# Sliding-window attention and a two-layer product on one core: full products for the first chunk, scores one unit at a time, and a stored order for every engine

## The chip, the cores and the metric

One core of a Trainium2 chip. The time is the device time of one execution in microseconds (us), median of the runs named. "Span" is the time from the first to the last instruction in the profiled execution, which lies 1.6 to 1.8 us below that run's own time. "Clock" is the granted clock of TensorE as a share of full speed. PE is TensorE, DVE is VectorE, ACT is ScalarE, POOL is GpSimd. Products of PE land in PSUM (tiles named ps); the other on-chip tiles lie in SBUF. An evacuation copies or combines a finished product out of PSUM. All quoted times are of runs in the fast state unless said otherwise; a run in the slow state is named and left out of the ratios.

## The reference, cut to what matters

```python
# q, k, v: 8 batches x 8 heads x 576 positions x 64;  w_in: 512x2048;  w_out: 2048x512
scores = scale * q @ k^T                       # ALiBi bias, causal window of 128
attn   = softmax(where(mask, scores + bias, -1e9))
x      = (attn @ v).transpose(0, 2, 1, 3).reshape(4608, 512)
h      = x @ w_in                              # "MoE1" in the texts below
g      = h * np.cos(h)
out    = g @ w_out                             # "MoE2"
```

## The kernel before

The kernel collects operations with their dependencies, then a scheduler gives each engine its order. PE needs attention (scores, then P·V, which multiplies the softmax weights by v), MoE1 and MoE2 for nine chunks of 512 tokens, and mixes them so that one fills the waits of another. MoE2 of every chunk is done with seven block products in place of eight, which needs sums of weight blocks (once) and of activation blocks (per chunk). Three of the four weight sums run on DVE, the fourth on GpSimd:

```python
def weight_sums():
    B11, B12 = w_out[:, 0:HF, 0:256], w_out[:, 0:HF, 256:512]
    B21, B22 = w_out[:, HF:NFC, 0:256], w_out[:, HF:NFC, 256:512]
    ...
    for o, i0, i1, r, w in (
            (T[1][:, :, :], B12, B11, up, [("T", 1)]),
            (T[2][:, :, :], B22, T[1][:, :, :], low + [("T", 1)], [("T", 2)]),
            (B12, B22, B12, low, up),                       # overwrites the weights
            (T[4][:, :, :], B21, T[2][:, :, :], low + [("T", 2)], [("T", 4)])):
        eng = "pool" if w == [("T", 4)] else "dve"
        op(eng, ... e.tensor_tensor(o, i0, i1, ALU.subtract) ...)
```

After the exponential, a mask is multiplied in on DVE:

```python
op("dve", lambda e, p=p, m=m: e.tensor_tensor(p, p, m, ALU.mult), ...)   # p, emask: SBUF, bf16
```

Two units of attention (a unit is a batch, a pair of heads and a group of rows) take their scores in one run on PE, in a mode that uses 64 of its rows (64*128 in the traces):

```python
scores(two, 0)                       # mode=1: both units in one run of matmuls
for n, u in enumerate(two):
    exps(u, n, 2 * phase + 2)
```

The order is made by a greedy list scheduler: at each step it takes, over all engines, the operation that can start first by modelled durations, with priorities where several can.

```python
while avail:
    ...
    soon = min(st for st, _ in cand)
    st, o = min(((st, o) for st, o in cand
                 if st <= soon + (40 if e != "pe" else 100 if o.pri < 5 else 10)),
                key=lambda c: (c[1].pri, c[1].seq))
```

The softmax here doesn't subtract the row's maximum and nothing guards it: scores larger than these inputs give would overflow.

## Time and profile before

| | before |
|---|---|
| median of 3 runs | 321.86 us (320.95 to 323.0) |
| span of the profiled run | 318.1 us, clock 0.987 (this run took 319.88 us) |
| PE busy | 293.0 us (92%), so 25.1 us idle |
| DVE, ACT, POOL busy | 259.3, 200.5, 100.9 us |

Here is one more view, the busy time by window, over four stretches of the span. The columns are: window, length, then busy time and number of instructions of PE, its weight loads, DVE, ACT and POOL, then clock, DMA share and GB/s.

```profile
37.00:58.00 21.00, 14.08 (x175) 9.64 (x174) 21.00 (x47) 11.81 (x16) 15.12 (x13) 0.84 1.31 110
58.00:80.00 22.00, 20.64 (x154) 11.98 (x154) 18.78 (x36) 15.29 (x23) 11.92 (x16) 1.00 1.93 140
80.00:284.00 204.00, 200.82 (x1954) 135.94 (x1964) 169.83 (x378) 138.60 (x195) 54.31 (x65) 1.00 1.09 112
284.00:318.10 34.10, 28.30 (x246) 23.44 (x245) 21.63 (x39) 5.81 (x11) 0.00 (x0) 0.98 0.26 86
```

Read length minus PE busy. PE idles 6.92 us in the first stretch, where DVE is full and the clock is 0.84 on average; 1.36 in the second, 3.18 in the long middle and 5.80 in the tail. The remaining 7.8 us lie before 37 us.

### The profile page before, as it was taken

How to read it: one execution, taken by the hardware profiler on the slowest of the kernel's cores; microseconds unless marked ns; L12 is line 12 of the kernel's file. 1: busy time of each engine (PE TensorE's matmuls, PEld its weight loads, DVE VectorE, ACT ScalarE, POOL GpSimd, SP SyncE). 2: the span in 40 equal slices, each digit the busy share in tenths (PEclk: the TensorE clock that was granted, in tenths of full speed). 3: DMA queues.
4: the chain of work that ended last, by engine and by line, in shares of the span. 5: the costliest groups of instructions: out<-in, count | busy, mean ns of one | idle time of the engine just before them, and what ended most of it. 6: DMA issues, size and time to landing. Idle time of an engine off the chain costs nothing.

```text
span 318.1 us, 7293 instructions
## 1 busy us (share of the span) xinstructions
PE 293.0 (92%) x2931; PEld 204.1 (64%) x2948; DVE 259.3 (82%) x569; ACT 200.5 (63%) x287; POOL 100.9 (32%) x123
## 2 busy tenths in 40 slices
PE   2899776998999998999999999999999999997995
PEld 2677545546754776548798855676476467666884
DVE  3798999799979698789988799789977586758653
ACT  6887755694859765686768667966887651632010
POOL 8960069727993812930392040000000000000000
PEclk9999959999999999999999999999999999999999
DMA  7999999999999999999999999623102001012122
GB/s 142 179 207 208 205 83 83 164 150 121 171 145 171 155 172 186 166 152 143 200 143 156 149 133 117 93 85 99 28 0 60 19 33 68 33 34 68 66 100 100
DMA packets 148865, 38.09 MB, mean 120 GB/s; under 512 B 133984, under 2 KB 148064, under 8 KB 148832
## 3 DMA queue, kind: packets, MB, share of 16 engines
q0 software_dynamic: 99344, 18.10, 75.0%
q1 hardware_dynamic: 49488, 19.54, 33.5%
q8 instruction: 23, 0.38, 0.5%
q14 instruction: 10, 0.08, 0.1%
HBM read 36.70 MB, written 9.44 MB: 145 GB/s over the span
## 4 chain that ended last, share of the span: by engine, by line
PE 56%; DMA 18%; POOL 12%; SPq 6%; DVE 5%; issue 2%; ACT 0%; POOLq 0%; DVEq 0%; ACTq 0%
PE ps L705 26%; PE ps L819 24%; DMA w_outb<-in_moe_w_out_dram 7%; SPq L378 6%; DMA qnat<-in_q_dram 5%; DMA kt<-knat 4%; DMA knat<-in_k_dram 2%; POOL knat L367 2%; POOL vp L357 2%; POOL qnat L367 2%; PE ps L513 2%; POOL wsum L756 2%; PE ps L598 1%; PE ps L601 1%; DVE p L567 1%
## 5 line engine op out<-in xcount | busy, mean ns | idle before, releaser
L705 PE MATMUL ps<-xT,w_inb 128*128 128x512 bf16 (+1 forms) x559 | 113.2, 355 | 1.0 <-issue 0.2
L711 ACT ACTIVATE cos<-ps,halfpi 128x512 f32<-128x512 f32 x128 | 81.7, 687 | 33.4 <-DVE gT L715 20.7
L715 DVE TENSOR_TENSOR gT<-ps,cos 128x512 f16<-128x512 f32 x128 | 81.6, 685 | 12.1 <-ACT cos L711 9.7
L705 PEld LDWEIGHTS ps<-xT,w_inb 128*128 128x128 bf16 x576 | 54.9, 98 | 49.6 <-DVE gT L715 1.1
L543 ACT ACTIVATE p<-ps 128x768 bf16<-128x768 f32 (+1 forms) x64 | 55.5, 915 | 28.5 <-PE ps L513 24.2
L819 PE MATMUL ps<-w_outb,gT 128*128 128x256 f16 x432 | 56.3, 275 | 2.2 <-DVE ob L843 1.7
L357 POOL DMA_DIRECT2D vp<-in_v_dram x40 | 34.0, 901 | 50.0 <-PE ps L601 30.2
L819 PEld LDWEIGHTS ps<-w_outb,gT 128*128 128x128 f16 x432 | 40.8, 98 | 9.9 <-DVE ob L843 2.0
L567 DVE TENSOR_TENSOR p<-p,emask 128x512 bf16<-128x512 bf16 (+1 forms) x96 | 43.7, 490 | 3.3 <-ACT p L543 3.0
L819 PE MATMUL ps<-wsum,gsum 128*128 128x256 f16 x288 | 38.8, 275 | 1.2 <-ACT ob L839 0.7
L819 PEld LDWEIGHTS ps<-wsum,gsum 128*128 128x128 f16 x288 | 27.1, 98 | 7.5 <-ACT ob L839 1.0
L367 POOL DMA_DIRECT2D qnat<-in_q_dram x30 | 25.5, 896 | 13.0 <-DMA qt<-qnat 8.1
L367 POOL DMA_DIRECT2D knat<-in_k_dram x30 | 25.5, 909 | 1.9 <-DMA kt<-knat 1.9
L513 PE MATMUL ps<-qt,kt 64*128 64x128 bf16 (+1 forms) x320 | 19.8, 252 | 5.2 <-DVE gT L738 2.0
L639 DVE TENSOR_TENSOR xnat<-ps,rec 128x256 bf16<-128x256 f32 x64 | 24.3, 419 | 0.2
L598 PE MATMUL ps<-vp,p 128*128 128x65 bf16 x256 | 18.8, 196 | 3.5 <-DVE p L567 2.2
L598 PEld LDWEIGHTS ps<-vp,p 128*128 128x128 bf16 x256 | 15.9, 99 | 8.4 <-DVE p L567 3.6
L513 PEld LDWEIGHTS ps<-qt,kt 64*128 64x128 bf16 x320 | 11.8, 98 | 12.1 <-issue 4.7
L819 PE MATMUL ps<-wsum,gT 128*128 128x256 f16 x144 | 18.2, 273 | 1.1 <-DVE krows L843 1.1
L779 DVE TENSOR_TENSOR gsum<-gT 128x1024 f16<-128x1024 f16 x18 | 12.3, 684 | 8.3 <-PE ps L819 8.3
L819 PE MATMUL ps<-w_outb,gsum 128*128 128x256 f16 x144 | 18.9, 273 | 0.0
L601 PE MATMUL ps<-vp,p 128*128 128x65 bf16 x192 | 17.5, 195 | 0.0
(69 smaller groups left out, 322.6 us busy)
## 6 DMA issues: line engine op xcount, KB each, us to landing
out_dram<-ob SPq DMA_DIRECT2D x32, 256.0 KB, 3.1
vp<-in_v_dram POOLq DMA_DIRECT2D x32, 128.0 KB, 9.3
qnat<-in_q_dram POOLq DMA_DIRECT2D x24, 128.0 KB, 9.3
knat<-in_k_dram POOLq DMA_DIRECT2D x24, 128.0 KB, 11.4
w_inb<-in_moe_w_in_dram POOLq DMA_DIRECT2D x4, 512.0 KB, 10.5
w_outb<-in_moe_w_out_dram POOLq DMA_DIRECT2D x4, 512.0 KB, 22.2
out_dram<-ob SPq DMA_DIRECT2D x8, 128.0 KB, 1.7
qrows<-in_q_dram POOLq DMA_DIRECT2D x1, 576.0 KB, 15.2
```

The lines of the kernel that those rows point to most:

```text
L357: op("pool", [lambda e, t=t, rows=rows: e.dma_start(vp[b % 2][0:rows, t, :, 0:64], v[b, :, 128 * t:128 * t + rows, :].rearrange("h p d -> ...
L367: fns.append(lambda e, t=t, rows=rows: e.dma_start(nat[which][b % 2][0:rows, t, :, :], src[b, :, 128 * t:128 * t + rows, :].rearrange("h p ...
L513: ins = e.matmul(ps[:, banks[x], c0:c1], keys_ap(b, x, pr, kc), query_ap(b, x, pr, qb, 128 * nb), start=True, stop=True)
L543: op("act", lambda e: e.activation(P[i][:, :, 0:hi], src_[:, :, 0:hi], ACTF.Exp, scale=0.125), w=held + [("P", i)], occ=920 if G else 691, ...
L567: op("dve", lambda e, p=p, m=m: e.tensor_tensor(p, p, m, ALU.mult), r=[("P", i), ("EM", h0), ("EM", h1)], w=[("P", i)] if n != 1 else [("P ...
L598: ins = e.matmul(o, P[i][:, x, d0:d0 + 128], V[:, kc, h, 0:65], start=True, stop=not two)
L601: ins = e.matmul(o, P[i][:, x, p0:p0 + 128], V[:, kc - 1, h, 0:65], start=False, stop=True)
L639: op("dve", lambda e: e.tensor_tensor(o, U[:, :, :, 0:64], rv[:, :, :, None].broadcast_to([128, 2, 2, 64]), ALU.mult), r=[("rec", n % 2)], ...
L705: op("pe", lambda e, kc=kc, c0=c0: e.matmul(ps[:, bank, c0:c0 + n], w_in[:, kc, 128 * fc:128 * fc + 128], xT[:, kc, (r0 + c0) % XR:(r0 + c ...
L711: op("act", lambda e: e.activation(cosb[ci][:, :], ps[:, bank, :], ACTF.Sin, bias=halfpi[:, 0:1]), r=["halfpi"], w=[("B", bank), ("cos", c ...
L715: op("dve", lambda e: e.tensor_tensor(gT[gi][:, fc, :], ps[:, bank, :], cosb[ci][:, :], ALU.mult), r=[("cos", ci)], w=[("B", bank), ("g", ...
L819: op("pe", lambda e, t=t, fc=fc, bk=bk: e.matmul(ps[:, bk, 256 * t:256 * t + 256], lhs(fc, t), rhs(fc), start=first and fc == 0 and (last ...
```

## The change

Its intent: the first chunk's MoE2 shall not wait for sums, scores shall be free to go one unit at a time, and the greedy order gives way to an order found beforehand by a local search on the schedule model (the kernel holds the finished table). The weight sum that overwrote a block of the weights gets its own buffer, since the full products read that block. Where an instruction of DVE writes what one of the few just before it on DVE reads (fewer than four back), it gets an explicit wait.

```diff
+STARTS = ( ...  # packed start times, one for each operation
+)
     def schedule(self):
-        ...                              # the greedy scheduler
+        raw, n = zlib.decompress(base64.b85decode(STARTS)), len(self.all)
+        code = 0
+        for i, o in enumerate(self.all):
+            code = (code + 256 * raw[i] + raw[n + i]) & 0xFFFF
+            o.start = code >> 1
             if len(o.eng) > 1:
+                e = "dve" if code & 1 else "act"
+                o.fn, o.eng = o.fn[e], (e,)
+        self.order = sorted(self.all, key=lambda o: (o.start, o.seq))
...
-                if data == ORDER or self.held(d, data, e):
+                near = data == WAR and e == "dve" and len(ops[e]) - d.nth < 4
+                if data == ORDER or (self.held(d, data, e) and not near):
                     continue
...
-                    (B12, B22, B12, low, up),
+                    (T[3][:, :, :], B22, B12, up + low, [("T", 3)]),
...
+        FAST = set(range(1, NCH))
+        def moe2_plain(c):               # 4 row tiles x 16 products of 512 columns
+            ...
         def moe2(c):
+            if c not in FAST:
+                moe2_plain(c)
+                return
...
+        SINGLE = True
-                if phase < 0:
+                if phase < 0 or SINGLE:
                     for n, u in enumerate(two):
                         scores([u], n)
-                        exps(u, n, 0)
+                        exps(u, n, 2 * phase + 2)
                         mask(u)
```

More of the change, by code (lines that the diff above doesn't have):

```diff
@@ L1 @@
+import base64
 import math
+import zlib
 from contextlib import ExitStack
@@ L25 @@
 ENG = ("pe", "act", "dve", "pool", "sp")
+STARTS = (
+    "c-p;I3vg3a8qO_MkCz>|JyvZ_(l(r4TQ-Io!li9`bJK*jA-rOF^pSRJLoHA!Rf@RSf`SzaEk!^<K`Nl)QV|?sl(meD=&*`)R"
+    "bbs&U2)fOQCM{pS9vV7x%=OnN0X*VnQ_caPX5<<{NMTi??l7MvL^8HD+6dU6Hvh}E4pga1f7wecnCbFm;<V;e*K}9A`Ehj%7"
+    "oNjjjCugJ>g~jVM)GbTcnp6WZdAqy?t58aZJwuS;pYdm#3zG+Wt`5>LNc5Wtccsy>J5~GiQTaG7+0!{c|~5Wg=k@tq|C@mr="
+    "(EuN;x=&s*ey0U8VlQK}pXZeUJa4|5)zQJ&ZviMg07equx9L0Fh8fu`vLO%nr=<_e%ip2Qz}vQVy9sT}_R`zadZ4<0gN{v{="
+    "W-Z%|&0qWF0D5QQxEaez1V`Bzmi8@)RzM_EZ?K_aVX-{}}_+iv;k^9=@va*Gr(J&Xm;t$dhbBz_qTs34!PmJYqe@omzjMNij"
+    ">#N1cs$>S3`^$I-20aRM*&ptfz#>d<G|Cs^)!Muiz?ixGOH^j>)iE9*i%1&l32hap$_x{<{Cpk8_I+<e(?;`v97TNoe#O+=h"
+    "nfOnw5qunZ1Z1>5}7El;`&~eeqe#CM;))VX@eFfYWFZ!a^&9yIegwrOn}UKVw>z*+mg{-idKijpuh}NG8e9V?co~>Jr#^5_V"
+    "r~3ep#7FS^4uNU!7O4ev5-)=UAkEQmen0VWQHCVC}eQVEU4dCWhXAuU;qyAb?tqO;L_|)dIhA%xRgJ6U$*<lq2riKS1UK*@|"
+    "wJ<8#x~4M{1vpRgRqU3}YkcB<R$aJz?{v8?~#gzH#hrTkr`y!;+!^aB?*I2;aJE)3vzyLYve-)J`$k`3;a#JM=>b#Bh=mW<Y"
+    "d!p;Ay{!p)-#9idIGxyDI5<b1T{LM%5`H%1_-6ma?<w<Y(hT-q>I~^0qk@On-3t3%Nm`{6_V^I!#S4eZYML8ypZ6;zqL0FFv"
+    "wo8A*gs_CO&n~PqBZBc{)-*{*n8O@Pk|w-~ScDQ;GSa%1fW&qpUeb|7kPuE1>+uI*M8fhVw<6Vz+MG{gn2XrvBypb-#9^E%U"
+    "Qk?!<s9NV2tQUvP?C5WB%-dec*+mW_R%v-|F!<^zn=0vw7;Hot!{NCOORIM?Oii=WEPT#%a)NXqwslN>wIrqfw^=|ZE<oos5"
+    ")H&;r15~Eh(Mu<Uiu(>SR*Q&m?2BG5<n=0_23W+OoHNinQs&g$sQe&V>b=hw3TMc`(hSmJa2F9L`k+OsPOEFJq$T3LHW?-CU"
+    "F-aJ<3t(+ch+#W|Sc=X2Pk?;Q1GA_N=6cVM(h$L+R>?cyEy@KPc%>^zr8T$c4{+YIqCEV)@~fSAe74H%b{NMC}bNPGdd;qw}"
+    "~4*WZ53tu2m=XfkUKt*jWCuB;=m~-7DiTk&c*3~bPDHTa?&rUO(Nqt(sWZ@9^9QtPCj75$HvMqC5dEIYm-Bv4<LV`|C_Lh4^"
+    "T3QFH{d=M(uk*{?YqJyiG_0iV@A3Hl<g=J-bJm*+;U?6Z3JytUVLTLJS-dsMkJuv12@D5kkv?S7-52(z+Z5bB{3azFjuF&VV"
+    "zPA+%2EtwFxe4ik=AO1nxf*X3fj_XIzwm^m(kzPPjY%+axI;aKeTNJ-zg0T@BI9gFcyiMVC8Af+ZB+lTPdav@e%GN0bmF3$h"
+    "-tB;LO%FB?3pim%%czbj^`U{i{zcS){AO#C?tw5KD?zzr;P|q2t+5N=|!saz^>xV+=F*DU~yn#F1M*Xx#P0<L4ArtF!9H@Vm"
+    "&JDVu!n6=Oc{;%(f$-L6Lc!?fP`?=gV#u9^df+-KYy+ei9_9A1F_n`1VwiUtZnBO!KUP_dY>J#}tBwC%PpLJB~_79gw@6}ef"
+    "lp1>#_vE!|6!QcSiCG4G3YgH*xor6|jc7*kFC`N<$I91AU3Lw-bHn?!hqj{}mDfsieY+Qgn;#587G3J+Ygm)Ltq?r&o3uD0~"
+    "-Y;Nm6ss`alPTT=MQ<ow%v&(6D&{%d;`|R5xE${~SH<oT>+er1gv>{glgrCnhtj)eWve*MyT^MQU%LMJb^MD5q0z4UHsyK!&"
+    "AzQ<`dDypulY(}l~v)c*Ei+?t_d~Er@6my=lrDiJy;#L``cXK?%|$hloEjpIcr4dSrX7~i1lR@_LY|c4$87zABA)x%4i6yE*"
+    "K7%m+p-ZdKDd=K{)TG1AWjx0X2C_tDVLMh{zzmfk;sLj76LxwOfa`@JlITw_PueIEXwf%0%nMv4J(x4N|MZbnq<@w+2_4n3s"
+    "xJx=3ARQo!b-*14)+LYY!3Frx=J&LHNqK(`#rrB`{0x*4MDrYd2m3{^{?sTLmUxY5<Hck`O-rbD^@y~ABwr!yC4=M{D0A37%"
+    "UU8J|EkR$-$qc5d$L#Vz&Usb(D|Hd5vdTLGgKisdmkG_6?b=;wkbA6sMJDUo20(3Zpv9fCih(swmu*~s>!7;LMT0TkmPHkS*"
+    "R;CP9KSpBiGo4>H^vn}UBy8JQ#IAkD0n%ftsaClwlJ>qaqB8IOh{NsTXnuk5Yq5gj)nAC&!nD<U#Cl+YT=5NH6?5Kn=v~{IV"
+    "xR`9%mRkUz-`ziRSMWhCye)D3!PrU;c}DoDKNI9SUOTly4oB5?1j8<G@jjGU7u<!9g%JP=eHF{6X~2Aj9bV%8Lv3wt?=?al`"
+    "?+zJ8!L9ej~gk+^UX4DGx3^=U(foAFVu~H7kAH<bcm?9?~4mc;qaMM?$I%xw7k`yBO724j_kKk$H0fGHr5@{Y*yW#v7a1QPy"
+    "WcZ%3@HWuEH7qa<!O2nVYPItstQx#O*8aEKBO;*%vVXyfhNN$iofaD0hBZvx50R9pgHhjRl!<`SJ{oSTaID#Wj<bF1uogpqm"
+    "2DHaSBchtf<-ufdCm<(b<32$^r;t}uh_WQo6vmZ3A>UfzhYbc+!PkAW!b<7hgrhQ_?lhdA~!*+M(m=DiI4pSssC3W}XuC(`~"
+    "*^XUc*=b~L#NlB-_9%Cc9J=R1-f4)vYa&U^v+h@GqYR;=kOq(9wN?#cOTNZRY3d&%9SD$W1_GNueJ@Z^`_z4V;CU3auDdWV0"
+    "nrm$*{}njTn+RF6fZqPCl-v8o`;Zh=PY=`tMfN-?RUjHpQgChAl}L0Hd@#<8#md<{}JPOYCX--EQ2^X$NU%0ckKM$z_|&s5r"
+    "HMRM7YJqa#?N4f$a+vPw5RI5@ESODOk*be26`mwD$W55P*+Sve;q@T)mB7s5-RP!>roSJ3uo5k?>mUD{y+Vcsgg;0a~S8U+3"
+    "20hwy6)OTB=~a?!hj+D+2Cdddmnc8rO|nqkBEl$eaMXR=h+bO<0>$Ki2?DT{p_O;qf{m;O*a3DWi9DfP{iH%zcSdaT;-JJ#}"
+    "U)E!~e?fDJc4q}!kZW|oegtqk-z0cAt47A!E2og@E52M2ro>ej;o$6ejzY_7vdxo;`LiPkJxW=Y^dfQjZ!X_4N3oLF*Nc%Ev"
+    "HHZ|ZC^;*jDYpLuQs?Z+"
+)
@@ L32 @@
                  "preds", "succs", "npred", "ready", "start", "end", "proc", "idx", "waits",
-                 "clock", "need", "val")
+                 "clock", "need", "val", "nth")
 class Plan:
-    SWITCH = 95
-    TABLE = 1330
-    WIRE0 = 3450
-    BEGIN = {"pe": 1000, "act": 2100, "dve": 1000, "pool": 1330, "sp": 1000}
-    COLD = 18500
     def __init__(self, nc, ctx):
@@ L91, in schedule @@
     def schedule(self):
-        free = dict(self.BEGIN)
-        wire = {e: self.WIRE0 for e in ENG}
-        mode, table = 0, 0
-        tables = sorted({o.table for o in self.all if o.table is not None})
-        left = {t: sum(o.table == t for o in self.all) for t in tables}
-        avail = []
-        def reach(o, e):
-            t = 0
-            for d, data in o.preds.items():
-                if data == ORDER or self.held(d, data, e):
-                    t = max(t, d.start + d.occ)
-                elif d.dma is None and d.eng[0] == e:
-                    t = max(t, d.end + 28)
-                else:
-                    t = max(t, d.end + (53 if e == "pe" else 36))
-            return t
@@ L109, in schedule @@
-        for o in self.all:
-            if o.npred == 0:
-                avail.append(o)
-        order = []
-        while avail:
-            phase = next((t for t in tables if left[t]), None)
-            best = None
-            for e in ENG:
-                cand = []
-                for o in avail:
-                    if e not in o.eng or (o.table is not None and o.table != phase):
-                        continue
-                    st = max(free[e], reach(o, e))
-                    if e == "pe" and o.mode != mode:
-                        st += self.SWITCH
-                    cand.append((st, o))
-                if not cand:
-                    continue
-                soon = min(st for st, _ in cand)
-                st, o = min(((st, o) for st, o in cand
-                             if st <= soon + (40 if e != "pe" else 100 if o.pri < 5 else 10)),
-                            key=lambda c: (c[1].pri, c[1].seq))
-                key = (st, o.pri, o.seq)
-                if best is None or key < best[0]:
-                    best = (key, e, o)
-            (st, _, _), e, o = best
-            avail.remove(o)
-            if o.table is not None and o.table != table:
-                st += self.TABLE
-            if len(o.eng) > 1:
-                o.fn, o.occ, o.lat = o.fn[e], o.occ[e], o.lat[e]
-                o.eng = (e,)
-            o.start = st
-            if e == "pe" and st < self.COLD:
-                o.lat += o.occ
-                o.occ *= 2
-            free[e] = st + o.occ
-            if o.dma is not None:
-                other = "sp" if e == "pool" else "pool"
-                begin = max(wire[e], st + 2300)
-                both = min(o.lat, max(0, wire[other] - begin))
-                wire[e] = begin + o.lat + both
-                wire[other] += both
-                o.end = max(wire[e], st + o.occ + 1400) + 500
-            else:
-                o.end = st + o.lat
-            if e == "pe":
-                mode = o.mode
-            if o.table is not None:
-                table = o.table
-                left[o.table] -= 1
-            order.append(o)
-            for s in o.succs:
-                s.npred -= 1
-                if s.npred == 0:
-                    avail.append(s)
@@ L166, in schedule @@
-        assert len(order) == len(self.all)
-        self.span = max(o.end for o in order)
-        self.order = sorted(order, key=lambda o: o.start)
-        rank = {id(o): i for i, o in enumerate(order)}
-        self.order.sort(key=lambda o: (o.start, rank[id(o)]))
+        raw, n = zlib.decompress(base64.b85decode(STARTS)), len(self.all)
+        assert len(raw) == 2 * n
+        code = 0
+        for i, o in enumerate(self.all):
+            code = (code + 256 * raw[i] + raw[n + i]) & 0xFFFF
+            o.start = code >> 1
+            if len(o.eng) > 1:
+                e = "dve" if code & 1 else "act"
+                o.fn, o.eng = o.fn[e], (e,)
@@ L184, in emit @@
             for d, data in o.preds.items():
-                if data == ORDER or self.held(d, data, e):
+                near = data == WAR and e == "dve" and len(ops[e]) - d.nth < 4
+                if data == ORDER or (self.held(d, data, e) and not near):
                     continue
@@ L200, in emit @@
             o.clock = dict(known[e])
+            o.nth = len(ops[e])
             ops[e].append(o)
@@ L273, in bass_alibi_sliding__then__act_gcu_kernel @@
         HF = NFC // 2
-        T = {n: sb(f"wsum{n}", [128, HF, 256], F16) for n in (1, 2, 4)}
+        T = {n: sb(f"wsum{n}", [128, HF, 256], F16) for n in (1, 2, 3, 4)}
         Sg = {n: sb(f"gsum{n}", [128, HF, 256], F16) for n in (1, 2, 4)}
@@ L286, in bass_alibi_sliding__then__act_gcu_kernel @@
         NX = 8
-        xnat = [sb(f"xnat{i}", [128, 256]) for i in range(NX)]
+        xbuf = sb("xnat", [128, NX, 256])
+        xnat = [xbuf[:, i, :] for i in range(NX)]
         xtl = [sb(f"xtail{i}", [64, 512]) for i in range(2)]
@@ L641, in norm, with norm_two, x_pe_two, f @@
                r=[("rec", n % 2)], w=[("B", ub), key], occ=340, lat=425, pri=0)
+        def norm_two(set_, n):
+            rc = rec[n // 2 % 2]
+            U = ps[:, UB[0]:UB[0] + 2, 0:260].rearrange("p u (g c) -> p u g c", c=65)
+            rv = rc[:, 0:8].rearrange("p (u g) -> p u g", u=2)
+            i = n % NX
+            o = xbuf[:, i:i + 2, :].rearrange("p u (g d) -> p u g d", g=4)
+            held = [("B", x) for x in UB]
+            op("dve", lambda e: e.reciprocal(rv, U[:, :, :, 64]),
+               w=held + [("rec", n // 2 % 2)], occ=110, lat=192, pri=0)
+            op("dve", lambda e: e.tensor_tensor(
+                o, U[:, :, :, 0:64], rv[:, :, :, None].broadcast_to([128, 2, 4, 64]), ALU.mult),
+               r=[("rec", n // 2 % 2)], w=held + [("xnat", i), ("xnat", i + 1)], occ=606, lat=691,
+               pri=0)
+        def x_pe_two(set_, n):
+            (b, pr, G), _ = set_[0]
+            i = n % NX
+            def f(e):
+                ins = None
+                for k_ in range(2):
+                    for r in range(2):
+                        ins = e.transpose(
+                            ps[:, UB[k_], :].bitcast(BF16)[:, 768 + 128 * r:896 + 128 * r],
+                            xnat[i + k_][:, 128 * r:128 * r + 128], ident[:, :])
+                return ins
+            t0 = S * b + 256 * G
+            held = [("B", x) for x in UB]
+            o = xT[:, pr:pr + 2, t0 % XR:t0 % XR + 256]
+            src_ = ps[:, UB[0]:UB[0] + 2, :].bitcast(BF16)[:, :, 768:1024]
+            op("pe", f, r=[("xnat", i), ("xnat", i + 1), "ident"], w=held, occ=240, lat=410, pri=0)
+            op(("act", "dve"),
+               {"act": lambda e: e.activation(o, src_, ACTF.Copy),
+                "dve": lambda e: e.tensor_copy(o, src_)},
+               w=held + xkeys(pr, t0, 256) + xkeys(pr + 1, t0, 256), occ={"act": 490, "dve": 390},
+               lat={"act": 591, "dve": 480}, pri=0)
         def xkeys(pr, t0, n):
@@ L780, in g_sums @@
                        r=r, w=w, occ=62 + 1068 // NG, lat=150 + 1068 // NG, pri=4)
+        def moe2_plain(c):
+            gi = c % 2
+            for t in range(4):
+                tg = 4 * c + t
+                bank = OB[tg % 2]
+                oi = tg % NOB
+                for fc in range(NFC):
+                    op("pe", lambda e, t=t, fc=fc, bank=bank: e.matmul(
+                        ps[:, bank, :], gT[gi][:, fc, 128 * t:128 * t + 128], w_out[:, fc, :],
+                        start=(fc == 0), stop=(fc == NFC - 1)),
+                       r=[("g", gi, fc, t // 2), ("wo", fc // 4)], w=[("B", bank)], occ=216, lat=379,
+                       pri=6)
+                op(("act", "dve"),
+                   {"act": lambda e, bank=bank, oi=oi: e.activation(
+                       ob[oi], ps[:, bank, :], ACTF.Copy),
+                    "dve": lambda e, bank=bank, oi=oi: e.tensor_copy(ob[oi], ps[:, bank, :])},
+                   w=[("B", bank), ("ob", oi), ("ob", oi, 0), ("ob", oi, 1)], occ={"act": 490, "dve": 606},
+                   lat={"act": 591, "dve": 691}, pri=6)
+                row = CH * c + 128 * t
+                op("sp", [lambda e, oi=oi, row=row: e.dma_start(out[row:row + 128, :],
+                                                                ob[oi])],
+                   r=[("ob", oi)], dma=f"st{oi}", occ=330, lat=750)
         def moe2(c):
+            if c not in FAST:
+                moe2_plain(c)
+                return
             gi = c % 2
@@ L806, in moe2 @@
                      "P5": (made(1), comb(1)), "P6": (made(2), comb(2)),
-                     "P7": (raw(0, 1), block(0, high))}
+                     "P7": (raw(0, 1), comb(3))}
             def bank(role, t):
@@ L833, in read @@
                                    for t in ts]
-                if out_ is not None and c == 0:
+                if out_ is not None:
                     w += [("ob", out_)]
-                if out_ is None and c == 0:
+                if out_ is None and c == min(FAST):
                     w += [("qB", w_, x) for w_ in ("q", "k") for x in range(2)]
@@ L873, in moe2 @@
             step("P3", "Z", False, (None, "u2", 1))
+        PAIRN = False
+        SINGLE = True
         ucount = [0]
@@ L897, in attention @@
                     after = []
+                    (b, pr, G), _ = set_[0]
+                    if (PAIRN and phase >= 0 and len(set_) == 2 and set_[1][0] == (b, pr + 1, G) and set_[0][1] == UB[0]
+                            and ucount[0] % 2 == 0):
+                        n = ucount[0]
+                        ucount[0] += 2
+                        norm_two(set_, n)
+                        if (S * b + 256 * G) // CH > phase + 1:
+                            x_dma(set_[0][0], n)
+                            x_dma(set_[1][0], n + 1)
+                        else:
+                            x_pe_two(set_, n)
+                        continue
                     for u, ub in set_:
```

## The prediction

> **What bounds the kernel now.** I read the page first, for the engines and for the slices of the span.
>
> ```profile
> PE 293.0 (92%) x2931; PEld 204.1 (64%) x2948; DVE 259.3 (82%) x569; ACT 200.5 (63%) x287; POOL 100.9 (32%) x123
> ...
> PE   2899776998999998999999999999999999997995
> ...
> PEclk9999959999999999999999999999999999999999
> DMA  7999999999999999999999999623102001012122
> ```
>
> TensorE (PE) is the bound: 92% busy, 9 in almost every slice. Its idle time is 318.1 - 293.0 = 25.1 us. Three places show it: the start (nothing for 5.6 us), slices 4 to 7, and the end. In slice 5 the granted clock is also halved. The DMA row says something else to keep in mind: the transfers are dense until about 195 us. So I cut slices 4 to 7 with the busy time by window, 1 us at a time (columns: window, length, then busy time and instruction count of PE, weight loads, DVE, ACT, POOL, then clock, DMA share, GB/s).
>
> ```profile
> 37.00:38.00 1.00, 0.26 (x3) 0.00 (x0) 1.00 (x3) 0.73 (x2) 0.00 (x0) 1.00 1.26 209
> 38.00:39.00 1.00, 0.00 (x0) 0.00 (x0) 1.00 (x2) 0.98 (x2) 0.00 (x0) 1.00 1.22 210
> 39.00:40.00 1.00, 0.51 (x8) 0.31 (x8) 1.00 (x3) 0.52 (x2) 0.00 (x0) 1.00 1.44 189
> 40.00:41.00 1.00, 0.00 (x0) 0.00 (x0) 1.00 (x3) 1.00 (x2) 0.00 (x0) 0.68 2.22 162
> ...
> 44.00:45.00 1.00, 1.00 (x18) 0.85 (x19) 1.00 (x3) 0.00 (x0) 1.00 (x1) 0.50 0.29 18
> ...
> 49.00:50.00 1.00, 0.00 (x0) 0.00 (x0) 1.00 (x6) 0.15 (x1) 1.00 (x2) 1.00 0.00 0
> ```
>
> From 37 us PE has nothing to do while DVE is full in every window: the first chunk's MoE1 is done, and its MoE2 (the seven-product scheme) cannot start before DVE has made sums of weights and of activations. The order of the work there is in the chain of waits:
>
> ```profile
> 14.72 21.32 DMA w_outb<-in_moe_w_out_dram
> 36.14 1.23 DVE wsum L756
> 37.37 1.80 DVE gT L738 x3
> 39.16 0.60 DVE gsum L779
> 39.76 0.60 DVE gT L779
> 40.36 0.81 DVE gsum L779 x2
> 41.18 0.31 issue
> 41.49 1.23 DVE wsum L756
> 42.78 0.10 issue
> 42.88 5.94 POOL wsum L756
> ```
>
> So a late weight transfer, then a serial chain on DVE, holds PE. By the timeline of PE the idle gaps here are 2.05 (before 39.31), 1.60, 0.52, 1.78 (before 50.30) and 0.69 us (before 55.17): 6.6 us. The clock is about 0.5 from 40.7 to 47.9 us; PE was busy about 6 us of it, so about 3 us more are lost. **The stretch from 37 to 58 us costs some 9.7 us.** After it PE idles little: 1.15 us at 77.5, 0.7 at 117 to 120, 1.11 at 124.1, 2.0 between 287 and 292, and 3.1 us at the very end, when only the last evacuation and store run.
>
> [...] PE did 0.77 us of work between 37 and 41 us and the clock fell to 0.50. So removing the gap returns the slow clock too. [...] while the GpSimd weight sum ran (42.88 to 48.83), one mask multiplication on DVE (128x512, usually about 0.4 us) took 3.39 us, and the 1.78 us gap of PE ends with that group. [...] In the trace a run of scores for two units of the full kind takes 0.55 us; its columns alone are 0.43 us (2 units x 512 columns at 216 ns per 512), so about 0.12 us for going in and out.
>
> **The change, part by part.** Instruction counts are from the listing of the changed order against the old one.
>
> 1. *Chunk 0's MoE2 plain.* Removed: 112 matmuls of 256 columns, at 109 ns (77 in 8.41 us in the chain) 12.2 us. Added: 64 of 512 columns at 216 ns, 13.8 us. **PE: +1.6 us.** DVE loses 8 activation sums (0.60 us apart) and 5 evacuations, and gains one copy: about 7.5 us less, just where it is full. PE no longer needs those sums: plain products follow MoE1 as soon as weights land. By the listing 20 of them (4.3 us) and two runs of scores stand between the end of MoE1 (37.26) and the wait for the last weight quarter, so PE reaches that wait at about 42 us; the quarter lands at about 41.5, by the DVE sum that waited for it. The gaps of 2.05, 1.60 and 0.52 go, and with them the half clock: **-7.2 us.**
> 2. *The GpSimd sum stays,* with the same inputs, so it again starts near 42.8 us and can again shut out a mask for 3 us. PE now has products left as filler; my hand replay with the durations above leaves about 2 us of waiting of the 2.5 us in the two later gaps: **-0.5 us.**
> 3. *Scores unit by unit.* The same matmuls; 42 runs of scores in place of 37, and 93 mode changes in place of 83, so 5 extra entries at 0.12: **+0.6 us.**
> 4. *Order from the table; extra waits of DVE on itself.* DVE instructions that wait for DVE's own semaphore rise from 106 to 149 listed rows[...], on an engine with 18% to spare, so off the path. In the last two chunks the new order mixes products of different banks matmul by matmul, which is aimed at the gaps of 1.68 and 0.31 us; in the middle it can save at most the 1.15, 0.7 and 1.11. Of these 5 us I give it half: **-2.3 us.** The start and the tail do not change.
>
> Sum: +1.6 - 7.2 - 0.5 + 0.6 - 2.3 = **-7.8 us**, from 321.86 to about 314.1.
>
> **Rivals.**
>
> *A. The loads of batch 2 become the wall.* Keys of batch 2 land at 75.39 us and PE uses them at 75.59: no slack today. Their chain starts at the GpSimd sum (42.88), which does not get earlier; issue, landing and transposes follow it:
>
> ```profile
> 42.88 5.94 POOL wsum L756
> 48.83 4.21 POOL qnat L367 x5
> 53.03 3.41 POOL knat L367 x4
> 56.44 7.92 DMA knat<-in_k_dram
> 64.37 6.18 SPq L378
> 70.60 4.79 DMA kt<-knat
> ```
>
> If PE gained 8 us it would simply wait there. Against it: the listing puts 74 units of MoE2 (512-column equivalents) before those scores, where the old order had 39.5, which is 7.5 us more PE work. Then PE arrives at 75.6 - 7.7 + 7.5, about 75.4: just in time. The same holds at batch 4, which waited 1.11 us for its keys. If the filler did not suffice, up to 3 us of gain are lost: 317.
>
> *B. The lock bites harder.* [...] PE runs out of filler, idles over 3 us and drops to half clock again: 4 to 5 us of the gain go, 318 to 319. For it: 3.39 us measured now. Against it: PE still has over 40 plain products then, 9 us.
>
> *C. DVE becomes the bound* through the self waits and an order with no slack: every small deviation on the chip then stops PE. It would show as many gaps of 0.1 to 0.5 us; 316 to 320.
>
> *D. The table does better* and removes nearly all gaps between 58 and 300 us: 309 to 311.
>
> **Range and chances.** Centre 314.1. D gives the lower edge, B and C the upper: 309 to 319 for 8 in 10. The limit for 2% is 315.4, just 1.3 us above my centre; with a deviation of about 3.7 us that makes roughly 0.62 faster, 0.35 within 2%, 0.03 slower, the last only if B and C meet.
>
> **What would show it right or wrong.** PE busy nearly full from 37 to 45 us and the clock at 1.00 in slices 5 and 6: step 1. A mask of DVE of about 3 us near 45 to 49: step 2. First scores of batch 2 at 75 to 77 us with under 1 us of wait: rival A held off; a wait for the transposed keys of over 1.5 us there or at batch 4: A. Half clock anywhere after 20 us: B. DVE above 85% with PE under 93%: C. PE should be 94 to 95% of some 310 us. The prediction is wrong if the stretch is not the place of the gain, or if more than 3 us appear in the middle of the span.

## The result, and the profile after

The changed kernel took 313.2 us (310.54 to 313.73, 4 runs), the kernel before 321.4 in the same rounds. Ratios in this document are the record's: fast runs of one kernel over fast runs of the other in the same rounds, so not quite the ratio of the medians quoted. Here it is 0.9722 [0.9655, 0.979]: faster. The point of the prediction, 314.1, is 0.9 us off.

The page after, the engines' line and the rows of slices for PE, clock and DMA:

```profile
PE 296.0 (95%) x2900; PEld 197.7 (63%) x2900; DVE 258.5 (83%) x555; ACT 201.2 (65%) x290; POOL 99.9 (32%) x123
...
PE   2899986999999999999999999999999999999996
...
PEclk9999995999999999999999999999999999999999
DMA  7999999999999999999399999931221210110214
```

PE is 95% busy of 311.6 us, and the small dents of before are gone. One place is left, slices 5 and 6 (counted from 0), and the half clock is still there, in slice 6. The same four stretches, busy time by window:

```profile
37.00:58.00 21.00, 17.21 (x141) 8.59 (x139) 16.01 (x28) 11.70 (x16) 15.06 (x14) 0.84 1.47 132
58.00:80.00 22.00, 22.00 (x180) 11.78 (x178) 17.31 (x37) 14.71 (x24) 11.35 (x14) 1.00 1.98 158
80.00:284.00 204.00, 202.83 (x1976) 134.40 (x1975) 181.56 (x394) 140.62 (x196) 53.89 (x65) 1.00 1.05 112
284.00:311.60 27.60, 24.73 (x212) 20.23 (x210) 16.42 (x29) 6.03 (x11) 0.00 (x0) 1.00 0.23 77
```

PE idle fell from 6.92 to 3.79 us in the first stretch, whose mean clock is 0.84 as before. It fell from 1.36 to 0 in the second, from 3.18 to 1.17 in the middle and from 5.80 to 2.87 in the tail: 9.4 us less in all. PE busy rose by 3.0 us. Together that is the 6.5 us by which the span fell (the medians differ by 8.2 us, since the profiled run of the kernel before, 319.88 us, was a quick one). So two thirds of the idle time saved lies after 58 us, where the prediction had put the smaller part.

The first stretch, 1 us at a time:

```profile
40.00:41.00 1.00, 1.00 (x12) 0.41 (x11) 0.27 (x1) 0.99 (x2) 0.00 (x0) 1.00 2.19 162
44.00:45.00 1.00, 1.00 (x12) 0.41 (x8) 1.00 (x1) 1.00 (x2) 1.00 (x1) 1.00 0.36 23
45.00:46.00 1.00, 0.30 (x2) 0.00 (x0) 1.00 (x1) 0.93 (x2) 1.00 (x1) 1.00 0.58 221
47.00:48.00 1.00, 0.00 (x0) 0.00 (x0) 1.00 (x1) 0.00 (x0) 1.00 (x2) 0.71 0.00 0
49.00:50.00 1.00, 0.91 (x13) 0.74 (x13) 0.63 (x3) 0.00 (x0) 1.00 (x2) 0.50 0.73 47
```

From 37 to 45 us PE is full at full clock: the full products removed the old gaps. Then PE runs dry at 45.3, and at 47.42 us the granted clock falls from 1.00 to 0.50. The timeline of POOL and of PE, then the masks of DVE by tile (duration in ns: minimum, median, maximum; then first and last start):

```profile
42.94 4.87 POOL L763 TENSOR_TENSOR wsum<-w_outb,wsum 128x2048 f16<-128x2048 f16 x1 [21.80 <-DVE wsum L763]
49.09 0.33 PE L567 MATMUL ps<-vp,p 128*128 128x65 bf16 x3 [3.79 <-DVE p L536]
L536 DVE TENSOR_TENSOR p<-p,emask x12: 285/418/4273, 43.8 to 57.9; 128x512 bf16<-128x512 bf16 x4, 128x256 bf16<-128x256 bf16 x4, 128x1024 bf16<-128x1024 bf16 x4
```

One mask took 4.27 us, from 43.81 to 48.08, while GpSimd subtracted weight blocks (42.94 to 47.81); the median of the twelve masks is 418 ns. P·V needs the masked scores, so PE waited 3.79 us. By the trace's clock record the half clock lasted from 47.42 to 54.24 us. This is rival B of the prediction, which it had not expected to bite.

Of the four runs of the changed kernel, three have a clock of 0.989 and spans of 311.4 to 311.9. The fourth has a clock of 1.000 and a span of 308.8. An estimate from these: the half clock costs 2.6 to 3.1 us (by the trace about 2.6, since PE worked 5.15 us under it), and it came in three executions of four (clock 0.989).

### The profile page after: what moved, and what is told of

Same layout as the page of the kernel before. It is cut to its first block, busy times and chain, and to the rows that moved or that the text cites. A ratio compares the mean times of both kernels' runs of the same rounds, so it can differ in the third digit from the quotient of the medians.

```text
span 311.6 us, 7164 instructions
## 1 busy us (share of the span) xinstructions
PE 296.0 (95%) x2900; PEld 197.7 (63%) x2900; DVE 258.5 (83%) x555; ACT 201.2 (65%) x290; POOL 99.9 (32%) x123
## 4 chain that ended last, share of the span: by engine, by line
PE 73%; DVE 11%; DMA 8%; POOL 4%; issue 1%; ACT 1%; POOLq 0%; ACTq 0%; DVEq 0%
PE ps L712 33%; PE ps L853 27%; DMA w_outb<-in_moe_w_out_dram 8%; PE ps L482 3%; DVE p L536 3%; PE ps L797 3%; PE ps L567 3%; DVE gsum L787 2%; DVE gT L722 2%; PE ps L570 2%; PE ps L674 1%; POOL vp L326 1%; DVE gT L787 1%; DVE wsum L763 1%; POOL krows L307 1%
## 5 line engine op out<-in xcount | busy, mean ns | idle before, releaser
L712 PE MATMUL ps<-xT,w_inb 128*128 128x512 bf16 (+1 forms) x576 | 123.4, 355 | 0.2 <-ACT p L512 0.2
L536 DVE TENSOR_TENSOR p<-p,emask 128x512 bf16<-128x512 bf16 (+2 forms) x96 | 46.2, 502 | 2.8 <-ACT p L512 1.9
L853 PE MATMUL ps<-wsum,gT 128*128 128x256 f16 x256 | 40.4, 273 | 0.0
L853 PE MATMUL ps<-w_outb,gT 128*128 128x256 f16 x256 | 35.5, 273 | 0.0
L853 PEld LDWEIGHTS ps<-w_outb,gT 128*128 128x128 f16 x256 | 24.4, 98 | 6.4 <-issue 0.5
L853 PEld LDWEIGHTS ps<-wsum,gT 128*128 128x128 f16 x256 | 24.1, 98 | 5.9 <-DVE krows L877 0.6
L853 PEld LDWEIGHTS ps<-wsum,gsum 128*128 128x128 f16 x256 | 23.6, 98 | 5.6 <-issue 0.5
L567 PE MATMUL ps<-vp,p 128*128 128x65 bf16 x256 | 18.8, 196 | 5.0 <-DVE p L536 4.7
L853 PE MATMUL ps<-w_outb,gsum 128*128 128x256 f16 x128 | 21.3, 273 | 0.0
L797 PE MATMUL ps<-w_outb,gT 128*128 128x512 f16 x64 | 19.1, 407 | 0.0
```

The costliest lines, as they stand in the source:

```text
L567: ins = e.matmul(o, P[i][:, x, d0:d0 + 128], V[:, kc, h, 0:65], start=True, stop=not two)
L712: op("pe", lambda e, kc=kc, c0=c0: e.matmul(ps[:, bank, c0:c0 + n], w_in[:, kc, 128 * fc:128 * fc + 128], xT[:, kc, (r0 + c0) % XR:(r0 + c ...
L797: op("pe", lambda e, t=t, fc=fc, bank=bank: e.matmul(ps[:, bank, :], gT[gi][:, fc, 128 * t:128 * t + 128], w_out[:, fc, :], start=(fc == 0 ...
L853: op("pe", lambda e, t=t, fc=fc, bk=bk: e.matmul(ps[:, bk, 256 * t:256 * t + 256], lhs(fc, t), rhs(fc), start=first and fc == 0 and (last ...
```

## The experiments

Two questions were open. Does the GpSimd subtraction really cost the time of the gap, and by which mechanism? The theory to be tested comes from the mask of 4.27 us above and is called the lock: the GpSimd subtraction, which reads SBUF, holds up a mask, which has two SBUF inputs, PE starves, and its clock falls. The rivals are that DVE just has too much to do there, that any GpSimd work beside the masks does it, and that the subtraction is needed as a brake on the loads behind it. The second question is where the rest of the gain comes from: the full products, the single scores or the order. Eleven kernels ran; all gave correct results.

### The fourth weight sum, in other places

**On DVE, late.** The fourth sum goes to DVE and behind the masks, where DVE has time. Beside the masks GpSimd then only issues transfers (41.58 to 45.16 us by its timeline).

```diff
+        next(o for o in self.all if o.w == (("T", 4),)).start = 2270
...
-                eng = "pool" if w == [("T", 4)] else "dve"
+                eng = "dve"
```

> The fourth weight sum is taken from GpSimd and made on VectorE, late, where VectorE has gaps (about 60 us). Theory L (the GpSimd sum shuts a two-input mask of VectorE out; PE then idles 3.79 us and loses about 2.8 us more to the halved clock): both go, the longest mask falls from 4.27 us to about 0.3 to 0.5, no gap of PE over 1 us between 40 and 60 us, clock 1.00 there, and the time falls from 313.2 by about 6.5 to 306.7. Rival R (the wall is the loads of batch 2, keys landing near 75 us): PE only arrives earlier and waits for the keys, gain at most about 3, time 310 or more. Rival N (the order after it has no slack, and small waits eat the gain): 309 to 312.

Measured: 307.16 us (307.05 to 307.28), ratio to before 0.9538 [0.947, 0.9606]; before stood at 323.3 on that chip over 7 runs, one of them slow (324.54) and left out of the ratio; the other six have a median of 321.8. Span 305.5, clock 1.000. The page's lines and the masks of DVE by tile:

```profile
PE 292.1 (96%) x2882; PEld 196.6 (64%) x2900; DVE 255.7 (84%) x556; ACT 201.1 (66%) x290; POOL 95.0 (31%) x122
...
PE   2799999999999999999999999999999999999996
```

```profile
L537 DVE TENSOR_TENSOR p<-p,emask x12: 284/418/693, 43.6 to 51.9; 128x512 bf16<-128x512 bf16 x4, 128x256 bf16<-128x256 bf16 x4, 128x1024 bf16<-128x1024 bf16 x4
```

The longest mask is 0.69 us, the gap and the half clock are gone (clock 1.000 in all four runs), and 6.0 us of median with them (313.2 to 307.16; the two medians come from different calls).

**On DVE, early.** The same sum on DVE, ahead of the masks, to see whether its place matters.

```diff
+        next(o for o in self.all if o.w == (("T", 4),)).start = 1730
...
+                eng = "dve"
```

> As t4_dve_late, but the fourth sum directly behind the third on VectorE, so that the masks come about 1.15 us later (from 45.0 in place of 43.8). It asks how much slack the full products give PE there. PE ran out of them at 45.3 us in the changed kernel and the first products of attention need two units' masks: expected a gap of 0.5 to 1.2 us near 45 to 47 us, clock still 1.00, 307.5 to 308.5. If the table's order has more slack than that: 307.1 as late. If it has no slack and the gap brings the half clock back: 310.

Measured: 308.13 us (307.69 to 308.45), ratio 0.9588 [0.9554, 0.9622], clock 1.000. PE's timeline has one wait:

```profile
46.49 0.25 PE L568 MATMUL ps<-vp,p 128*128 128x65 bf16 x3 [1.19 <-DVE p L537]
```

PE waits 1.19 us for the masks, about the length of one sum (1.23 us on DVE). So a sum of one and a quarter us ahead of the masks costs about 1 us; the subtraction on GpSimd cost 6.

**On GpSimd, doubled.** A second subtraction of the same size, from the same inputs, runs right behind the first on GpSimd and writes a buffer that chunk 1 overwrites. If the subtraction shuts out the masks, the gap doubles.

```diff
         weight_sums()
+        op("pool", lambda e: e.tensor_tensor(Sg[4][:, :, :], w_out[:, HF:NFC, 0:256], T[2][:, :, :],
+                                              ALU.subtract), r=[("T", 2), ("wo", 2), ("wo", 3)],
+           w=[("S", 4, 0), ("S", 4, 1), "gate"])
```

> The suspected cost doubled: the same sum is made a second time on GpSimd right behind the first (its result is overwritten later, the output stays right). Theory L: VectorE masks are shut out for about twice as long (two masks of over 3 us, or one of about 8), PE idles 6 to 8 us in place of 3.8, time 317 to 320. If the long mask has another cause: no change of it, 313 to 314, unless the loads, 4.9 us later, hold PE at batch 2.

Measured: 316.59 us (316.23 to 316.94), ratio 0.983 [0.976, 0.9901]. The timelines of POOL and PE:

```profile
43.29 4.87 POOL L766 TENSOR_TENSOR wsum<-w_outb,wsum 128x2048 f16<-128x2048 f16 x1 [22.18 <-DVE wsum L766]
48.13 4.21 POOL L984 TENSOR_TENSOR gsum<-w_outb,wsum 128x2048 f16<-128x2048 f16 x1
53.30 0.32 PE L570 MATMUL ps<-vp,p 128*128 128x65 bf16 x3 [7.69 <-DVE p L539]
```

The gap went from 3.79 to 7.69 us, almost exactly by the length of the second subtraction. The time rose by 3.4, a little less than the gap: the half clock again lasted 6.83 us (50.25 to 57.08), but PE worked only 3.78 us under it in place of 5.15.

**Three GpSimd writes in its place.** The sum is on DVE, late. GpSimd instead clears three buffers at the old place, which only writes SBUF. This tells two rivals apart. If any GpSimd work beside the masks hurt, the masks would be long again. If the subtraction's only service had been to hold back the loads that follow it on GpSimd (rival A), this kernel holds them back as well.

```diff
+        for i in (1, 2, 4):
+            op("pool", lambda e, i=i: e.memset(Sg[i][:, :, :], 0.0), r=[("T", 2)],
+               w=[("S", i, 0), ("S", i, 1), "gate"])
```

> As t4_dve_late, but GpSimd, where the sum was, waits for the same VectorE sum and then only writes (three memsets of 128x2048), so that the loads of batch 2 start about as late as they did (near 48 us). Theory L with reading as the cause: no mask over 0.7 us although GpSimd computes; the gap at 45 to 49 us is gone. If the loads are no wall: about 306.7 as t4_dve_late. If they are (R): PE waits 2 to 3 us for transposed keys near 73 to 75 us, and the time is about 309. If any GpSimd computation blocks VectorE: the gap stays and the time is 313.

Measured: 307.93 us (307.6 to 311.46), ratio 0.9591 [0.9481, 0.9701]. POOL's timeline, the masks by tile, and two lines of PE's timeline:

```profile
43.05 5.53 POOL L986 MEMSET gsum<- 128x2048 f16 x3 [21.95 <-DVE wsum L767]
```

```profile
L540 DVE TENSOR_TENSOR p<-p,emask x12: 285/419/693, 44.0 to 51.9; 128x512 bf16<-128x512 bf16 x4, 128x256 bf16<-128x256 bf16 x4, 128x1024 bf16<-128x1024 bf16 x4
```

```profile
73.75 0.50 PE L486 MATMUL ps<-qt,kt 64*128 64x256 bf16 x8 [0.25 <-DMA kt<-knat]
...
123.18 0.51 PE L486 MATMUL ps<-qt,kt 64*128 64x256 bf16 x8 [0.85 <-DMA kt<-knat]
```

The writes took 5.53 us beside the same masks, and the longest mask was again 0.693 us, against 4.27 beside the subtraction, which reads SBUF: of these two kinds of GpSimd work only the one that reads held a mask. The loads behind it come late enough that PE waits 0.25 us for the keys of batch 2 and 0.85 us for those of batch 4. So rival A is real, and its price is 0.8 us by the medians (307.16 to 307.93), 0.4 by its run without a half clock (307.60, clock 0.999): the profiled run also has a half clock from 15.30 to 18.71 us, long before the writes. One of the four runs took 311.46 at a clock of 0.994; I have no cause for it.

**On GpSimd, behind the loads.** The sum stays on GpSimd and is given a late place in the order.

```diff
+        next(o for o in self.all if o.w == (("T", 4),)).start = 2400
```

> The sum stays on GpSimd with the same operands, but behind the loads of batch 2, so at about 60 us, where VectorE mostly multiplies a PSUM by an SBUF operand (one SBUF input). Theory L: those run at their 0.69 us, the sum takes 4 to 6 us or shorter, no gap at 45 to 49 us, time about 306.7. If GpSimd blocks VectorE whatever its operands: some multiplication at 60 to 66 us takes over 3 us and PE idles there, time 310 to 313.

Measured: 312.19 us (310.63 to 313.18), ratio 0.9689 [0.9612, 0.9767]. The run missed its aim. The order moved, but the queue of GpSimd was empty there and nothing else held the sum back, so it ran only 2 us later, from 44.91 to 48.97, still beside the masks. The longest mask was 4.72 us, and PE's timeline shows the old wait:

```profile
49.28 0.32 PE L568 MATMUL ps<-vp,p 128*128 128x65 bf16 x3 [3.91 <-DVE p L537]
```

Here a later place in the order was not a later place in time, but for those 2 us.

**On GpSimd, held back by a dependency.** So the sum was made to wait for the last evacuation of chunk 0's output, which is past the masks. DVE then does multiplications that take one operand from PSUM.

```diff
+        t4 = next(o for o in self.all if o.w == (("T", 4),))
+        t4.start, t4.preds[self.all[474]] = 2400, DATA
```

> What t4_pool_late missed (relieved of its wait, GpSimd ran through the loads and made the sum at 44.9, among the masks again): the sum stays on GpSimd and now waits for the last evacuation of chunk 0, so that it runs from about 60 us, beside multiplications of VectorE with one operand in PSUM. Theory L with two SBUF inputs as the condition: no multiplication of VectorE longer than 0.75 us, no PE gap at 45 to 49 us, 307 to 308. If GpSimd blocks VectorE whatever its operands: one of 3 to 4 us near 60 to 65 us and PE idle there, 310 to 312.

Measured: 307.13 us (306.9 to 307.41), ratio 0.9561 [0.9528, 0.9595], clock 1.000, the same as on DVE. The timelines of POOL and DVE:

```profile
61.22 4.08 POOL L765 TENSOR_TENSOR wsum<-w_outb,wsum 128x2048 f16<-128x2048 f16 x1 [15.97 <-DVE ob L807]
```

```profile
62.23 2.48 DVE L724 TENSOR_TENSOR gT<-ps,cos 128x512 f16<-128x512 f32 x4 [0.58 <-ACT cos L720]
```

Four multiplications of one PSUM and one SBUF operand took 2.48 us beside the subtraction, 0.62 each from start to start, no longer than elsewhere (685 ns mean duration of that group in the changed kernel, overlapping a little). And the subtraction itself took 4.08 us, against 4.87 in the changed kernel, where a weight sum of DVE was still running as it began (42.68 to 43.90 us; t4_pool_late, among the masks, has 4.06). So the subtraction on GpSimd cost nothing beside these multiplications with one operand in PSUM (307.13 us, against 307.16 with the sum on DVE); among the masks, with two SBUF inputs, it held one for 4.27 us, or 4.72 in t4_pool_late.

### The parts of the change, under the old order

Four kernels take the changed kernel's operations and the old greedy scheduler; one takes the kernel before. The edits:

```diff
     def schedule(self):              # greedy_plain: the scheduler of before put back, and
-        SINGLE = True
+        SINGLE = False               # greedy_single: SINGLE = True
```

```diff
-                eng = "pool" if w == [("T", 4)] else "dve"
+                eng = "dve"          # before_t4_dve, greedy_plain_t4_dve, greedy_single_t4_dve
```

The extra waits of DVE on itself stay in all of these but the kernel before. In the greedy kernels the scheduler plans anew after each edit, so moving the sum also moves other work: only in the stored order does the sum move alone.

> Part 1 alone: chunk 0's MoE2 as full products (and the extra waits of VectorE on itself), scores still for two units, the order again from the old list scheduler. By the prediction's sum: +1.6 - 7.2 - 0.5 = -6.1 from 321.4, so 315. If most of the measured gain comes from the table's order instead: 318 or more. By the traces I lean to 316 to 318, since the mask is shut out here too and PE has then little filler.

Measured: 324.32 us (323.8 to 325.19), ratio 1.0099 [1.0066, 1.0133]. Full products alone make the kernel 1% slower under the old order (the interval lies above 1). The longest mask took 4.02 us beside the subtraction on GpSimd (42.67 to 46.73). PE's timeline shows the wait for it, and the tail as it was:

```profile
47.69 0.33 PE L641 MATMUL ps<-vp,p 128*128 128x65 bf16 x3 [3.96 <-DVE p L610]
...
292.89 1.92 PE L927 MATMUL ps<-w_outb,gT 128*128 128x256 f16 x16 [1.68 <-DVE ob L951]
295.56 1.16 PE L927 MATMUL ps<-w_outb,gT 128*128 128x256 f16 x9 [0.31 <-ACT qrows L947]
```

> Parts 1 and 3: as greedy_plain, scores unit by unit, order from the old scheduler. By the prediction +0.6 against greedy_plain for more entries into the scores' mode. The step from here to the changed kernel (313.2) is then what the table itself is worth: the prediction gave it 2.3 us, so 315.5; the traces, where the overhead after batch 2's first scores fell from 13 to 8 us, say about 5, so 318.

Measured: 328.08 us (327.5 to 329.42), ratio 1.022 [1.0181, 1.0258], 3.8 us more than with paired scores.

> The kernel before with only its fourth weight sum moved from GpSimd to VectorE (the old scheduler replans). If the lock cost the kernel before what its trace shows (the 1.78 us gap of PE that ends at the mask, part of it filled): 319 to 320.5 in place of 321.4. If the chain on VectorE of sums is what counts there, one more sum of 1.2 us on it makes it no better: 321 to 323. The gaps of 2.05 and 1.60 us and the half clock stay in both cases, and so does the time near 320: the lock becomes the main cost only once the other waits are gone.

Measured: 319.47 us (319.04 to 319.86), ratio 0.9945 [0.9915, 0.9976]. The longest mask is 0.69 us here, 3.39 in the kernel before. There the lock cost only 1.7 us: the gaps of 2.06 and 1.60 us before 41.47 us, in which PE waits for other work of DVE and ACT, stay without it, and so does the half clock (41.70 to 48.53 us).

> greedy_plain (full products for chunk 0, old scheduler, 324.3) with its fourth weight sum on VectorE. Theory L: its gap of 3.96 us before 47.7 us and the half clock behind it come from the same lock, so about 5 us come back: 318 to 320. Then the full products are worth little or nothing against the kernel before with the same move (319.5) unless the order is made for them. If the full products are a gain of their own of 6 us, as the prediction had it: 313 to 315. If the loss of greedy_plain is all in the later gaps: 323 to 324.

Measured: 315.64 us (315.48 to 315.8), ratio 0.9825 [0.979, 0.9859], clock 1.000. Without the lock the full products do gain, 3.8 us over the kernel before without the lock. Not all of the 8.7 us from 324.32 is the lock's: greedy_plain has a second half clock, from 115.47 to 118.88 us, after waits of PE of 0.30 and 1.42 us and within one of 0.25 us, and greedy_plain_t4_dve has none (about 1.6 us, an estimate: half of PE's busy time under it).

> All the operations of t4_dve_late (full products, scores unit by unit, fourth weight sum on VectorE), but in the old scheduler's order: what the table's order alone is worth with the lock out of the way. greedy_plain_t4_dve took 315.6; scores unit by unit cost 3.8 us under the old scheduler with the lock (61 entries into the scores' mode by the listing, in place of 38, at about 0.12 us, and small waits). So 318 to 320, and the table is worth 11 to 13 us. If the cost of single scores was itself an effect of the lock's gap: 315.5 to 316.5, and the table is worth 8.5.

Measured: 321.52 us (321.39 to 321.7), ratio 1.0024 [0.9964, 1.0084], clock 1.000; before stood at 320.68. Single scores under the old order cost 5.9 us here (on two chips).

All of it in one table. Medians in us; PE busy and idle from the profiled runs, where idle is the span less busy.

| operations and order | sum on GpSimd | sum on DVE | moving the sum saves | span = PE busy + idle, sum on GpSimd | the same, sum on DVE |
|---|---|---|---|---|---|
| before, greedy | 321.1 | 319.5 | 1.7 | 318.1 = 293.0 + 25.1 | 317.3 = 294.0 + 23.3 |
| full products, greedy | 324.3 | 315.6 | 8.7 | 322.1 = 296.5 + 25.6 | 314.1 = 293.5 + 20.6 |
| and single scores, greedy | 328.1 | 321.5 | 6.6 | 326.0 = 300.9 + 25.1 | 319.8 = 299.8 + 20.0 |
| and single scores, stored order | 313.2 | 307.2 | 6.0 | 311.6 = 296.0 + 15.6 | 305.5 = 292.1 + 13.4 |

The first three rows were taken on one chip, except 321.5. With the ratios to the kernel before in place of the medians, the step from the third to the fourth row is 1.022 to 0.9722 and 1.0024 to 0.9538, so about 5% (some 16 us) either way; by the medians it is 14.9 and 14.3.

Why single scores cost so much under the old order is seen in the groups of PE by line, where the scores of all units are one row. Columns: line, engine, operation, output and inputs, shape, count, then busy time in us, mean ns of one, and idle time before the group. First the kernel before:

```profile
L513 PE MATMUL ps<-qt,kt 64*128 64x128 bf16 (+1 forms) x320 | 19.8, 252 | 5.2 <-DVE gT L738 2.0 <-ACT p L543 1.9 <-DVE kt L476 0.9
```

Full products under the old order with the sum on DVE, paired scores and then single scores:

```profile
L556 PE MATMUL ps<-qt,kt 64*128 64x128 bf16 (+1 forms) x320 | 19.1, 245 | 2.5 <-DVE kt L519 0.9 <-ACT p L586 0.7 <-DVE rec L680 0.6
```

```profile
L556 PE MATMUL ps<-qt,kt 64*128 64x128 bf16 (+1 forms) x320 | 23.5, 255 | 2.9 <-DVE gT L796 1.6 <-DVE kt L519 0.9 <-DVE rec L680 0.5
```

And the changed kernel:

```profile
L482 PE MATMUL ps<-qt,kt 64*128 64x128 bf16 (+1 forms) x320 | 20.0, 249 | 1.2 <-DVE kt L445 0.9 <-ACT kt L444 0.3
```

The 320 matmuls are the same everywhere. From paired to single the listing of the orders has 38 and 62 entries into the 64-row mode, and the busy time rises by 4.4 us. About 1.1 us of that lies before 37 us, where the clock record begins its full clock later in the second run (at 17.30 us, in the first at 11.84) and where 4 more matmuls fall; from 60 us on, at full clock, it is 3.0 us for 20 entries, 0.15 each. The timeline of single runs says much the same: two units in one run take 0.50 us, each alone 0.34 us, so 0.18 us more for splitting a pair. This leaves out the wait ahead of the first score. From the start of the product before a run of scores to the start of the one behind it, the trace has 0.641 us for two units and 0.476 for one, with 0.109 us between two products of 256 columns: splitting costs 2 x (0.476 - 0.109) - (0.641 - 0.109) = 0.20 us. The stored order gets back to 42 entries and 20.0 us although the scores are single operations: it puts most pairs together again. It also has the least idle time before the scores, 1.2 us in place of 5.2.

## Why the prediction was right or wrong

The number was right. The sum behind it was wrong in two terms that cancelled, so that the point came within 0.9 us is luck.

- **What bounds the kernel, and step 1's mechanism: right.** PE is the bound. From 37 to 45 us it is full at full clock, as step 1 said; the gaps of 2.05, 1.60 and 0.52 us are gone. But the -7.2 us included the half clock, and that came back later. The prediction tied the half clock to these gaps and removed it with them. In the run, the mean clock from 37 to 58 us was 0.84 before and after; of the clock of 1.00 that the prediction wanted to see in slices 5 and 6, only slice 5 has it. The term was also read a little high: the clock record has the half clock from 40.36 to 47.19 us, not 40.7 to 47.9, and PE worked 5.1 us under it, so 2.6 us were lost, not 3. Once the lock is away, the stretch does give back what step 1 claimed: in t4_dve_late, PE idles 0.05 us there, at a clock of 1.00.
- **Step 2 failed: "my hand replay ... leaves about 2 us of waiting of the 2.5 us in the two later gaps: -0.5 us", and with it the argument against rival B, "PE still has over 40 plain products then, 9 us".** The products were there, but in the stored order PE had worked through what stood ahead of the P·V by 45.3 us, and next in that order was the P·V. The longest mask took 4.27 us, not 3.39: the masks came right behind the weight sums, and it ran beside the subtraction for 4.00 us of 4.87, in the kernel before (45.72 to 49.11, beside 42.88 to 48.83) for 3.11 of 5.94. The runs give the price: 6.0 us for the changed kernel, an estimate of its parts is a gap of 3.79 and a half clock of about 2.7, less a little that is made up later. The prediction had named 4 to 5 us for it and a time of 318 to 319.
- **Step 4 named the right cause, the order, but its term of -2.3 us was too small by some 4 us.** PE idle after 58 us fell by 6.3 us (1.36, 2.01 and 2.93 in the three stretches). In the tail, the prediction counted only gaps of 1.68 and 0.31; the tail's idle fell by 2.93, including what waited behind them. By the prediction's own sign, more than 3 us in the middle would make it wrong; from 58 to 284 us it was 3.4. Its other sign, that the stretch is the place of the gain, failed as well: of 9.4 us of idle time saved, the stretch gave 3.1. So rival D happened too, and B hid it. What the stored order is worth against the greedy one on the same operations is more still, 14 to 16 us, since under the greedy order single scores are a loss that the stored order first has to undo.
- **Step 3: the sign was right, the size of an entry was not.** It took 0.12 us for going in and out, by the columns of one run; splitting a pair costs 0.18 to 0.20. With 5 entries that makes 0.9 to 1.0 in place of 0.6. The rise of the scores' busy time was 0.2 over all (19.8 to 20.0), but both hold half-clock time; from 60 us on it was 0.6 for 4 more entries.
- **Plain products, +1.6 us of PE.** PE busy rose by 3.0 us from before to after, but both numbers contain slow-clock time. Without the half clock at 47 us, the stored order with the sum on DVE has 292.1. The term itself was not isolated.
- **Rival A: held off, as predicted.** First scores of batch 2 came at 79.44 us, with no wait, since keys had landed at about 75.2. The prediction had 75 to 77: PE came later because more work stood ahead of them and it lost time to the lock, not because of the keys. The kernel with three writes on GpSimd shows the limit: with PE faster by 6 us, keys cost 0.25 and 0.85 us of waiting.
- **Rival C: not seen.** DVE is 83% busy, and PE shows no swarm of small gaps: after 58 us it has four over 0.1 us, the longest 0.50. What the extra waits of DVE on itself cost could not be tried: the check before the chip reported a race in a kernel without them (a write to the buffer qrows against a read shortly before on DVE), and it was not run.

What stays open: which pauses of PE bring the half clock. It came with PE dry for 2.1 us in the changed kernel (45.3 to 47.42) and after the waits above in greedy_plain (the longest 1.42), and not after one of 1.19 us in t4_dve_early (clock 1.000); a rule was not shown. Open too is how the 14 to 16 us of the stored order divide. In the pair without the lock, 319.8 to 305.5, 7.7 us are busy time and 6.6 idle time. Of the busy time, 20 fewer entries at 0.20 explain 4.0 us, and the later full clock at the start of the greedy run up to 0.8; the rest was not traced to a cause. Paired scores under a stored order were not run either. Also open is what the seven-product form of chunk 0 would give with a stored order of its own; the table belongs to one list of operations and could not be reused for another.

## What to carry to other kernels

When a change removes the reason why the bounding engine idles, look at once at what the next wait would be, and let a run without the suspected wait decide: here an unchanged subtraction on GpSimd went from 1.7 us of cost to 6. Here it paid, by 6.0 us, to keep a GpSimd subtraction that reads SBUF away from the masks on DVE, which have two SBUF inputs. It was moved by a dependency (307.13 us) or to DVE (307.16), since a later place in the order alone moved it by 2 us only (312.19). A part of a change can be a loss alone (single scores under the greedy order, +3.8 to +5.9 us) and harmless under an order that was searched with it, so judge parts and order together.

The best versions found here are the changed kernel with the fourth sum on DVE, late (307.16 us), or on GpSimd behind chunk 0 (307.13 us): 4.4 to 4.6% below the kernel before.
